# Attention and two MLP layers on one core: the second layer regrouped into 1024, 1024 and 128 tokens

## The chip, the cores and the metric

The kernel runs on one core of a Trainium2 chip. TensorE does the matrix products, VectorE and ScalarE the elementwise work, and the DMA queues of SyncE and ScalarE move data between HBM and the on-chip memory. The metric is the device time of one execution in microseconds (us); lower is better. Three runs of the kernel before gave 831.91 to 832.73 us.

## The reference

Four sequences of 544 tokens (32 global and 512 local) go through attention with 8 heads of 64, and the 2304 rows of 512 through two layers, all in float32:

```python
out_g = sm(scale * q_g @ k_all.T) @ v_all            # 32 global queries see everything
out_l = sm(local window of +-32, and all global) @ v  # 512 local queries
x = concat(out_g, out_l) as (2304, 512)
x = leaky(x @ w_in, alpha) @ w_out                    # layer 1: 512 -> 2048 -> 512
h = x @ moe2_w_in                                     # layer 2: 512 -> 2048 -> 512
return (h * clip(h + 3, 0, 6) / 6) @ moe2_w_out
```

## The kernel before

A float32 product is made of three products of split operands (high times high, low times high, high times low), so each product of 128 by 128 weights is three matmuls, each with its own weight load. The hidden size of 2048 is 16 chunks j of 128; the inner size of 512 is 4 chunks c.

Layer 1 goes over five blocks of tokens, of 512, 512, 512, 256 and 384 columns (`blocks`, line 404); the last one holds a local half of 256 tokens and the 128 global tokens. In each block step s makes the hidden chunk s (`h_tile`, line 443, 12 matmuls), its activation and split (`act`, line 454), and two steps later (`LAG`) its share of the output (`y_tiles`, line 471). In between, `STEPS` (line 42) says how many steps of attention are issued after each step: first all local units, then four global units (line 318: scores `gs_ps`, exponentials, transposes `gpt_ps`, values `go_ps`). At the last step of a block the next block's attention output is transposed and split at once (`x_from_attention`, line 415). `SPLIT` spreads the preparation of layer 2's weights (`second_weights`) over the same blocks: it reads each 64-bit raw weight, makes float32, high and low parts and sums, and stores them to `wi_m` and `wo` in HBM.

Layer 2 (`second_layer`, line 769) takes the tokens in pairs of halves and uses a scheme with seven block products in place of eight. Before, there are two such groups (`twos`, line 632): 512 + 512 tokens and 384 + 384 tokens. For each, eight chunk pairs m run seven products of six matmuls (`product`, line 796, written to `k_ps`, width 512 or 384), and then seven sums over the hidden size (`summed`, line 874, written to `o_ps`, 256 columns each). The last 384 tokens (`rest`, line 633: local half and global tokens of block 4) go through a plain loop (lines 943 to 960): 16 times 12 matmuls of 384 columns and 9 of 512, with weights loaded once more. Weights come through a ring of eight buffers (`ahead`, line 700): six tiles are asked for ahead, and a tile's buffer is free again when its last matmul is done. `more` interleaves the next group's input splits into the sums (`MORE`, line 47).

The order on each engine is written by a scheduler that follows the program's priorities and its own estimate of times; `here` pins single instructions. Engines run their queues in order, SyncE's DMA queue too.

Of the kernel before, what the change touches and what calls it, by code (L numbers as in the profile page):

```python
# [25 lines left out]
W = 32  # L26
# [15 lines left out]
STEPS = [[2] * 4 + [1] * 16, [1] * 16, [1] * 16, [1] * 16, [0] * 16]  # L42
# [14 lines left out]
def fused_kernel(ctx, tc, qkE, vE, qgz, kN, vN, vgN, w1, w2, consts, out):  # L57
# [357 lines left out]
    def x_from_attention(pieces, xt, at):  # L415

        for hp in range(HP):
            t = bank("xt_ps")
            n = 0
            for piece in pieces:  # L420
                x = xo.pop(("g", hp) if piece == "g" else (*piece, hp))
                for i in range(1 if piece == "g" else 2):
                    nc.tensor.transpose(t[:, n:n + 128], x if piece == "g" else x[:, i, :], ident_sb)  # L423
                    n += 128
            split_x(t[:, :n], xt[hp][:, :, at:at + n], n)
# [3 lines left out]
    def active(bi, s):  # L429

        if bi:
            return [(0, width[bi], s)] if s < NJ else []
        if s < DELAY:
            return [(0, 256, s)]
        if s < 2 * DELAY:
            return [(256, 512, s - DELAY)]
        return [(0, 512, s - DELAY)] if s - DELAY < NJ else []
# [5 lines left out]
    def h_tile(xt, wts, parts):  # L443
        ps = bank("h_ps")
        for a, b, j in parts:
            k = 0
            for c in range(NC):
                for wl, xl in ((0, 0), (1, 0), (0, 1)):
                    nc.tensor.matmul(ps[:, a:b], lhsT=wts[j][:, 0, wl, 128 * c:128 * c + 128], rhs=xt[c][:, xl, a:b],  # L449
                                     start=k == 0, stop=k == 3 * NC - 1)  # L450
# [3 lines left out]
    def act(layer, ps, parts):  # L454
# [3 lines left out]
        if layer == 0:  # L458
            nc.scalar.activation(t[:, a:b], ps[:, a:b], AF.Relu, scale=-1.0)  # L459
            for c, d, j in parts:  # L460
# [10 lines left out]
    def y_tiles(layer, y, g, wts, parts, lanes=False):  # L471
        for a, b, j in parts:
# [3 lines left out]
            for (wl, gl), c in steps:  # L476
                first = a == 0 and j == 0 and (wl, gl) == (0, 0)
                last = j == NJ - 1 and (wl, gl) == (0, 1) and (not lanes or b == 512)
                if layer == 0:
                    nc.tensor.matmul(y[c][:, a:b], lhsT=wts[j][:, 1, wl, 128 * c:128 * c + 128], rhs=g[:, gl, a:b],  # L480
                                     start=first, stop=last, skip_group_check=lanes)
# [3 lines left out]

    def evacuate(y, c, n, tags=("t",)):
        r = work.tile([128, 512], F32, tag=tags[c % len(tags)], name="ev", bufs={"t": TB, "z": ZB}[tags[c % len(tags)]])
        if c % 2:
            nc.vector.tensor_copy(r[:, :n], y[:, :n])
        else:  # L490
            nc.scalar.copy(r[:, :n], y[:, :n])
        return r

# [138 lines left out]
    twos = [([(1, 0, 512)], [(2, 0, 512)]), ([(0, 0, 384)], [(0, 384, 128), (3, 0, 256)])]  # L632
    rest = 4
# [15 lines left out]
    def inputs(two, bt, keep=lambda x: x):  # L649
# [13 lines left out]
        for c in range(2):  # L663
# [23 lines left out]
                ("22", (3, 0))]  # L687

    stream = {"todo": [], "got": {}, "n": -1}

    def plan_stream():

        for n in range(len(twos)):
            stream["todo"] += [("in", n, m, kind) for m in range(NP) for kind in (0, 3, 2, 1)]
            stream["todo"] += [("sum", n, i, k) for i in range(len(PRODUCTS)) for k in range(NP // 2)]
        n = len(twos)
        for j in range(NJ + LAG):
            stream["todo"] += [("in", n, j // 2, j % 2)] * (j < NJ) + [("out", n, 0, j - LAG)] * (j >= LAG)

    def ahead(n):  # L700

        while stream["todo"] and len(stream["got"]) < n:
# [8 lines left out]
            if key[0] == "in" and key[1] < len(twos) and key[3] == 1:  # L711
                half = in_parts[key[2]][:, 1].rearrange("p (h c) -> p h c", h=2)[:, :, 256:512]
                nc.sync.dma_start(out=t.bitcast(F32)[:, :, 256:512], in_=half)
            elif key[0] == "in":
                nc.sync.dma_start(out=flat, in_=in_parts[key[2]][:, key[3]])
            elif key[0] == "out":
                nc.sync.dma_start(out=flat, in_=out_parts[:, key[3] // 2, key[3] % 2])
            else:
                kind, half = PRODUCTS[key[2]][1]
# [8 lines left out]
    def act2(src, g, n=512):  # L728
        t = work.tile([128, 512], F32, tag="t", name="t", bufs=TB)[:, 0:n]
        nc.scalar.activation(t, src, AF.Relu, bias=half_sb, scale=1.0 / 6.0)  # L730
        nc.vector.scalar_tensor_tensor(out=t, in0=t, scalar=1.0, in1=src, op0=ALU.min, op1=ALU.mult)
# [245 lines left out]
    for bi in range(len(blocks)):  # L977
# [5 lines left out]
        for s in range(end + LAG):  # L983
# [30 lines left out]
            if last and s >= 2:  # L1014
                next(more, None)
# [77 lines left out]
```

## Time and profile before

| what | us |
|---|---|
| median of 3 runs | 832.2 |
| profiled execution, its own time | 831.75 |
| its span, first to last instruction | 829.9 |
| TensorE busy | 812.1 (98%) |
| VectorE busy | 585.1 (70%) |
| ScalarE busy | 427.4 (51%) |

The span is the profile's clock: times in its rows count from the span's start. Matmul durations overlap in the records, so the time of a run of matmuls is read from the chain, where each piece ends where the next begins. The rows below are named by group in the prediction.

### The profile page before, as it was taken

Reading aid. Unit: us, or ns where it says so; the run is one execution under the profiler, and the core shown is the slowest. Engines: PE = TensorE matmul, PEld = TensorE weight load, DVE = VectorE, ACT = ScalarE, POOL = GpSimd, SP = SyncE. Lnnn points to the kernel's source line nnn. Section 1 sums busy time; section 2 is a strip of 40 time slices with the busy share of each in tenths; the row PEclk is TensorE's granted clock in tenths of the full one; section 3 lists DMA queues with packets and bytes.
Section 4 is the critical chain, followed back from the end, with each engine's and each line's share of the span. In section 5 each row is a group of like instructions: output and inputs, shape, how many; then the busy total and the mean of one; then the engine's idle time right before and its main releaser. Section 6 shows DMA issues by size and latency. Waiting matters only on the chain.

```text
span 829.9 us, 17685 instructions
## 1 busy us (share of the span) xinstructions
PE 812.1 (98%) x6940; PEld 724.3 (87%) x6940; DVE 585.1 (70%) x1283; ACT 427.4 (51%) x929; POOL 0.2 (0%) x4
## 2 busy tenths in 40 slices
PE   6999999999999999999999999999999999999997
PEld 4788888888888888788899988889999999999996
DVE  4998996477878777776688847778857778854221
ACT  5887995445556664465445434434542435532222
POOL 0000000000000000000000000000000000000000
PEclk9899999999999999999999999999999999999999
DMA  9985674347869767787595655666676878788871
GB/s 332 338 282 194 242 255 149 103 180 247 291 233 314 249 239 267 244 316 242 182 291 191 193 187 191 194 214 200 215 242 210 281 248 291 240 285 260 280 253 66
DMA packets 72866, 195.67 MB, mean 236 GB/s; under 512 B 7120, under 2 KB 18384, under 8 KB 72784
## 3 DMA queue, kind: packets, MB, share of 16 engines
q1 hardware_dynamic: 72688, 194.42, 69.5%
q8 instruction: 55, 0.90, 0.5%
q14 instruction: 27, 0.22, 0.1%
q10 hardware_dynamic: 96, 0.13, 0.1%
HBM read 152.05 MB, written 42.47 MB: 234 GB/s over the span
## 4 chain that ended last, share of the span: by engine, by line
PE 92%; ACT 3%; DVE 2%; DMA 2%; issue 0%; SPq 0%; ACTq 0%; DVEq 0%
PE y_ps L480 22%; PE h_ps L449 22%; PE o_ps L884 17%; PE k_ps L801 16%; PE h_ps L953 4%; PE o_ps L739 4%; DMA qk_t<-in_qkE 2%; PE s_ps L208 2%; PE o_ps L254 2%; PE pt_ps L241 1%; ACT p L230 1%; PE xt_ps L423 1%; PE gs_ps L346 1%; PE go_ps L391 1%; DVE z L121 0%; PE gpt_ps L373 0%
## 5 line engine op out<-in xcount | busy, mean ns | idle before, releaser
L480 PE MATMUL y_ps<-g,wt 128*128 128x512 f32 (+2 forms) x1008 | 206.3, 353 | 1.7 <-ACT g L467 1.7
L449 PE MATMUL h_ps<-xt,wt 128*128 128x512 f32 (+2 forms) x1008 | 204.3, 352 | 2.3 <-DVE xt L410 1.5
L449 PEld LDWEIGHTS h_ps<-xt,wt 128*128 128x128 f32 x1008 | 170.1, 191 | 24.7 <-DVE xt L410 2.4
L480 PEld LDWEIGHTS y_ps<-g,wt 128*128 128x128 f32 x1008 | 167.5, 189 | 25.6 <-ACT g L467 2.1
L884 PE MATMUL o_ps<-ws,gh 128*128 128x256 f32 x784 | 139.4, 283 | 0.0
L801 PE MATMUL k_ps<-bt,ws 128*128 128x512 f32 (+1 forms) x672 | 135.1, 362 | 0.0
L801 PEld LDWEIGHTS k_ps<-bt,ws 128*128 128x128 f32 x672 | 121.2, 188 | 13.0
L884 PEld LDWEIGHTS o_ps<-ws,gh 128*128 128x128 f32 x784 | 120.8, 192 | 0.1
L884 PE MATMUL o_ps<-ws,gl 128*128 128x256 f32 x392 | 107.0, 283 | 0.0
L814 ACT CAST gh<-far 128x1024 fp32r<-128x1024 f32 (+1 forms) x56 | 52.8, 942 | 62.5 <-PE o_ps L884 58.2
L815 DVE TENSOR_TENSOR gl<-far,gh 128x1024 fp32r<-128x1024 f32 (+1 forms) x56 | 60.9, 1088 | 33.0 <-ACT gh L814 32.8
L884 PEld LDWEIGHTS o_ps<-ws,gl 128*128 128x128 f32 x392 | 73.5, 192 | 0.0
L461 DVE SCALAR_TENSOR_TENSOR t<-t,c_sb,h_ps 128x512 f32<-128x512 f32 (+2 forms) x84 | 53.5, 641 | 27.9 <-ACT t L459 27.7
L459 ACT ACTIVATE t<-h_ps 128x512 f32<-128x512 f32 (+2 forms) x84 | 42.6, 512 | 45.0 <-PE h_ps L449 43.9
L468 DVE TENSOR_TENSOR g<-t,g 128x512 fp32r<-128x512 f32 (+2 forms) x84 | 49.1, 586 | 21.1 <-ACT g L467 18.6
L467 ACT CAST g<-t 128x512 fp32r<-128x512 f32 (+2 forms) x84 | 45.2, 538 | 35.3 <-DVE t L461 35.0
L786 ACT ACTIVATE t<-far,half_sb 128x512 f32<-128x512 f32 (+1 forms) x48 | 32.2, 671 | 50.8 <-DVE far L782 49.7
L230 ACT ACTIVATE p<-p,st 128x128 f32<-128x128 f32 x128 | 49.6, 390 | 12.6 <-DVE st L226 12.6
L121 DVE SCALAR_TENSOR_TENSOR z<-z,raw 128x512 uint32<-128x512 uint32 x64 | 43.6, 688 | 9.3 <-ACT z L116 6.0
L110 ACT ACTIVATE raw<-raw,quarter_sb 128x512 uint32<-128x512 uint32 x64 | 49.3, 772 | 1.2 <-DMA raw<-in_w 1.2
L123 DVE SCALAR_TENSOR_TENSOR z<-raw,z 128x512 uint32<-128x512 uint32 x64 | 43.4, 688 | 0.7
L953 PE MATMUL h_ps<-xt,ws 128*128 128x384 f32 x192 | 36.0, 336 | 0.0
(101 smaller groups left out, 858.4 us busy)
## 6 DMA issues: line engine op xcount, KB each, us to landing
ws<-wo SPq DMA_DIRECT2D x72, 512.0 KB, 4.2
raw<-in_w SPq DMA_DIRECT2D x64, 512.0 KB, 5.6
ws<-wi SPq DMA_DIRECT2D x64, 512.0 KB, 4.6
v_t<-in_vE SPq DMA_DIRECT2D x32, 512.0 KB, 7.1
qk_t<-in_qkE SPq DMA_DIRECT2D x32, 368.0 KB, 5.0
wi<-raw SPq DMA_DIRECT2D x16, 512.0 KB, 3.1
wi<-parts SPq DMA_DIRECT2D x16, 512.0 KB, 4.6
wo<-raw SPq DMA_DIRECT2D x16, 512.0 KB, 4.2
```

The lines of the kernel that those rows point to most:

```text
L110: here(nc.scalar.activation(low, low, AF.Relu, bias=quarter_sb, scale=0.9 * 2.0 ** -29))
L230: nc.scalar.activation(p[:, n, :], p[:, n, :], AF.Exp, bias=st[:, 1, n:n + 1], scale=-1.0, accum_out=st[:, 2, n:n + 1])
L449: nc.tensor.matmul(ps[:, a:b], lhsT=wts[j][:, 0, wl, 128 * c:128 * c + 128], rhs=xt[c][:, xl, a:b], start=k == 0, stop=k == 3 * NC - 1)
L461: nc.vector.scalar_tensor_tensor(out=t[:, c:d], in0=t[:, c:d], scalar=c1_sb[:, j:j + 1], in1=ps[:, c:d], op0=ALU.mult, op1=ALU.add)
L467: nc.scalar.copy(g[:, 0, a:b], t[:, a:b])
L468: nc.vector.tensor_tensor(out=g[:, 1, a:b], in0=t[:, a:b], in1=g[:, 0, a:b].bitcast(F32), op=ALU.subtract)
L480: nc.tensor.matmul(y[c][:, a:b], lhsT=wts[j][:, 1, wl, 128 * c:128 * c + 128], rhs=g[:, gl, a:b], start=first, stop=last, skip_group_check ...
L801: nc.tensor.matmul(bank, lhsT=wt[:, wl, at:at + 128], rhs=bt[x][:, c, xl, 0:w], start=first and k == 0, stop=k == 5, skip_group_check=True)
L814: nc.scalar.copy(hi, src)
L815: nc.vector.tensor_tensor(out=lo, in0=src, in1=hi.bitcast(F32), op=ALU.subtract)
L884: mm = nc.tensor.matmul(bank, lhsT=part[:, jp, 128 * c:128 * c + 128], rhs=wo[:, jp, 256 * wl:256 * wl + 256], start=opens, stop=k == NP / ...
L953: nc.tensor.matmul(h, lhsT=wt[:, wl, 128 * c:128 * c + 128], rhs=xt[c][:, xl, 0:w], start=k == 0, stop=k == 3 * NC - 1)
```

## The change

Layer 2 now has two groups of 512 + 512 tokens, the second one made of block 0 (512) and of the local halves of batch 3 (256 + 256). Only the 128 global tokens remain (`rest`), and they have no loop of their own: in the second group each chunk pair m, after its products, also multiplies the global tokens by its two unsummed weight tiles (`rest_in`, tokens as stationary operand, 12 matmuls of 256 columns), every second pair ends in an activation, and one pair later four transposes (`rest_turned`) and a split. The unsummed output weights are used during four of the sums (`REST_OF`): three are loaded there anyway, the fourth needs four loads at the end, with the last 24 matmuls (`rest_out`). The weight tiles of kind 0 and 1 are loaded in other pieces (halves of the inner size, runs of 1 KB), in the second group both halves of both.

In layer 1, the block of 256 columns goes in 8 steps of two hidden chunks, with one activation for both; `STEPS` issues three more attention steps in block 2, so the first global unit begins there; and `x_from_attention` is parted: transposes (`x_transposed`) at the block's last step as before, the splits (`x_split`) after its last `y_tiles`.

```diff
-STEPS = [[2] * 4 + [1] * 16, [1] * 16, [1] * 16, [1] * 16, [0] * 16]
+STEPS = [[2] * 4 + [1] * 16, [1] * 16, [1]*11+[2]*3+[1]*2, [2] * 8, [0] * 16]
...
+        if bi and width[bi] == 256:
+            return [(256 * i, 256 * i + 256, 2 * s + i, 0) for i in range(2)] if 2 * s < NJ else []
...
-    twos = [([(1, 0, 512)], [(2, 0, 512)]), ([(0, 0, 384)], [(0, 384, 128), (3, 0, 256)])]
-    rest = 4
+    twos = [([(1, 0, 512)], [(2, 0, 512)]), ([(0, 0, 512)], [(3, 0, 256), (4, 0, 256)])]
+    rest = x2[4][:, :, 256:384]
...
+    REST_OF = {0: (0, 0), 2: (1, 0), 4: (1, 1), 7: (0, 1)}
...
+            if key[0] == "in" and key[3] < 2:
+                own = in_parts[key[2]][:, 0:2].rearrange("p j (h t c) -> p (j h) t c", h=2, t=2)[:, :, key[3]]
+                n = 2 if key[3] == 0 and key[1] + 1 < len(twos) else 4
+                nc.sync.dma_start(out=flat.rearrange("p (jh c) -> p jh c", jh=4)[:, 0:n], in_=own[:, 0:n])
...
+        def rest_in(m, wts):
+            if m % 2 == 0:
+                hr["h"] = kept("hr_ps")
+            to = hr["h"].rearrange("p (m j k) -> p m j k", m=2, j=2)[:, m % 2]
+            k = 0
+            for c in range(NC):
+                for wl, xl in ((0, 0), (1, 0), (0, 1)):
+                    w = own_parts(wts[c // 2])[:, :, wl, 128 * (c % 2):128 * (c % 2) + 128]
+                    nc.tensor.matmul(to, lhsT=xr[0][:, xl, 128 * c:128 * c + 128], rhs=w, start=m % 2 == k == 0,
+                                     stop=k == 3 * NC - 1, skip_group_check=True)
+                    k += 1
...
+        def rest_turned(m):
+            t = kept("tr_ps")
+            for i in range(4):
+                nc.tensor.transpose(t[:, 128 * i:128 * i + 128], hr["t"][:, 128 * i:128 * i + 128], ident_sb)
+            split_x(t, gr[m // 2], 512)
+        def rest_out(y, i, k, wo):
+            kind, half = REST_OF[i]
+            for jp in range(2):
+                j = 2 * (2 * k + jp) + kind
+                for wl, gl in ((0, 0), (1, 0), (0, 1)):
+                    mm = nc.tensor.matmul(y[:, 256 * half:256 * half + 256],
+                                     lhsT=gr[j // 4][:, gl, 128 * (j % 4):128 * (j % 4) + 128],
+                                     rhs=wo[:, jp, 256 * wl:256 * wl + 256], start=i == k == jp == wl == gl == 0,
+                                     stop=i in (2, 7) and k == NP // 2 - 1 and jp == gl == 1, skip_group_check=True)
...
-            product(b0, 1, "21", ka, False)
+            b1 = take("in", n, m, 1)
+            product(b1, 0, "21", ka, False, True)
-            b1 = take("in", n, m, 1)
-            product(b1, 1, "t4", kc, False)
+            product(b1, 1, "t4", kc, False, True)
...
+                if end:
+                    if m and m % 2 == 0:
+                        rest_turned(m - 1)
+                    rest_in(m, (b0, b1))
...
+                    if end and i == k == 0:
+                        rest_turned(NP - 1)
+                    if end and i in REST_OF:
+                        rest_out(yr, i, k, wo)
...
-        n, w = len(twos), width[rest]
-        y = [kept("o_ps") for _ in range(w // 128)]
...
+            if end:
+                for k in range(NP // 2):
+                    rest_out(yr, len(PRODUCTS), k, take("sum", n, len(PRODUCTS), k))
+                rest_rows(yr, 1)
...
-                x_from_attention(blocks[bi + 1], xt_next, 0)
+                coming = x_transposed(blocks[bi + 1], 512 // width[bi + 1])
...
+            if s == end + LAG - 1 and not last:
+                x_split(coming, xt_next, 0)
```

TensorE's order at the start of the second group's products stands first (`k_ps` products, `hr_ps` the global tokens' hidden part, `tr_ps` its transposes). Before, the end of the first group's sums (`o_ps`) and then one run of products:

```order
L884 MATMUL o_ps<-ws,gh 128x256 x2
L884 MATMUL o_ps<-ws,gl 128x256
L801 MATMUL k_ps<-bt,ws 128x384 x328
L884 MATMUL o_ps<-ws,gh 128x256 x2
L884 MATMUL o_ps<-ws,gl 128x256
```

And after:

```order
L816 MATMUL k_ps<-bt,ws 128x512 x4
L768 MATMUL hr_ps<-ws,xr 128x256 x2
L816 MATMUL k_ps<-bt,ws 128x512 x6
L768 MATMUL hr_ps<-ws,xr 128x256 x16
L816 MATMUL k_ps<-bt,ws 128x512 x18
L768 MATMUL hr_ps<-ws,xr 128x256 x6
L816 MATMUL k_ps<-bt,ws 128x512 x24
L780 MATMUL tr_ps<-consts_sb,tr 128x128 x4
```

The global tokens' matmuls stand between the products, and the second pair's (the last 12 of the first 24) even stand ahead of all of that pair's own products.

VectorE's order at the end of block 1 (`xt` the next block's splits, `z`, `raw` and `parts` the weight preparation, `ev` the copies of block 1's output). Before:

```order
L410 TENSOR_TENSOR xt_3215<-xt_ps_3225,xt_3215 128x512
L410 TENSOR_TENSOR xt_3216<-xt_ps_3232,xt_3216 128x512
L410 TENSOR_TENSOR xt_3217<-xt_ps_3239,xt_3217 128x512
L548 TENSOR_TENSOR raw_3047<-z_3092,raw_3047 128x512
L113 TENSOR_SCALAR z_3260<-raw_3055 128x512
L1025 COPY ev_3321<-y_ps_2137 128x512
L121 SCALAR_TENSOR_TENSOR z_3260<-z_3260,raw_3055 128x512
```

And after:

```order
L121 SCALAR_TENSOR_TENSOR z_3252<-z_3252,raw_3055 128x512
L123 SCALAR_TENSOR_TENSOR z_3252<-raw_3055,z_3252 128x512
L410 TENSOR_TENSOR xt_3215<-xt_ps_3223,xt_3215 128x512
L549 TENSOR_TENSOR raw_3055<-z_3252,raw_3055 128x512
L410 TENSOR_TENSOR xt_3216<-xt_ps_3228,xt_3216 128x512
L558 TENSOR_TENSOR z_3252<-z_3252 128x256
L410 TENSOR_TENSOR xt_3217<-xt_ps_3233,xt_3217 128x512
L558 TENSOR_TENSOR z_3252<-z_3092,z_3252 128x256
L1039 COPY ev_3321<-y_ps_2137 128x512
L1039 COPY ev_3326<-y_ps_2139 128x512
```

The three later splits now have weight preparation ahead of them and between them.

TensorE's order where the first global unit runs. Before, in the block of 256 columns:

```order
L449 MATMUL h_ps<-xt,wt 128x256 x12
L480 MATMUL y_ps<-g,wt 128x256 x24
L373 MATMUL gpt_ps<-consts_sb,gp 128x128 x4
L374 MATMUL gpt_ps<-consts_sb,gp 32x128
L449 MATMUL h_ps<-xt,wt 128x256 x12
L373 MATMUL gpt_ps<-consts_sb,gp 128x128 x4
```

And after, in block 2:

```order
L490 MATMUL y_ps<-g,wt 128x512 x12
L459 MATMUL h_ps<-xt,wt 128x512 x12
L490 MATMUL y_ps<-g,wt 128x512 x15
L373 MATMUL gpt_ps<-consts_sb,gp 128x128 x4
L490 MATMUL y_ps<-g,wt 128x512 x6
L374 MATMUL gpt_ps<-consts_sb,gp 32x128
L459 MATMUL h_ps<-xt,wt 128x512 x12
L373 MATMUL gpt_ps<-consts_sb,gp 128x128 x4
```

Between a unit's scores and its first transposes there are now 39 matmuls of 512 columns, where there were 36 of 256.

## Rows read from the trace of the kernel before

**Rows 1.** The page: span, and each engine's busy time

```profile
span 829.9 us, 17685 instructions
...
PE 812.1 (98%) x6940; PEld 724.3 (87%) x6940; DVE 585.1 (70%) x1283; ACT 427.4 (51%) x929; POOL 0.2 (0%) x4
```

**Rows 2.** Chain that ended last, in order of time: start us, us, what

```profile
240.70 1.31 PE xt_ps L423 x12
...
484.04 74.62 PE k_ps L801 x329
558.65 69.11 PE o_ps L884 x576
...
640.66 56.86 PE k_ps L801 x328
697.52 51.83 PE o_ps L884 x432
...
766.31 2.10 PE h_ps L953 x12
768.42 2.08 PE o_ps L739 x9
...
818.66 6.18 PE o_ps L739 x27
```

**Rows 3.** Busy time by stretch: sums of group 1, products of group 2

```profile
559.00:629.00 70.00, 70.00 (x583) 70.00 (x582) 53.98 (x57) 33.12 (x40) 0.00 (x0) 1.00 0.68 215
...
640.00:698.00 58.00, 58.00 (x340) 58.00 (x339) 44.31 (x82) 25.44 (x46) 0.00 (x0) 1.00 0.83 274
```

**Rows 4.** Timeline of TensorE, 330 to 420 us, all its waits in brackets

```profile
352.98 1.71 PE L480 MATMUL y_ps<-g,wt 128*128 128x256 f32 x12 [1.47 <-ACT g L467]
...
355.61 1.69 PE L449 MATMUL h_ps<-xt,wt 128*128 128x256 f32 x12 [0.37 <-DVE gst L360]
357.65 0.66 PE L373 MATMUL gpt_ps<-consts_sb,gp 128*128 128x128 f32 x4 [0.36 <-ACT gp L361]
```

**Rows 5.** Timeline, 228 to 256 us: TensorE, then VectorE

```profile
245.76 5.61 PE L449 MATMUL h_ps<-xt,wt 128*128 128x512 f32 x24
...
238.11 0.75 DVE L260 TENSOR_TENSOR xo<-o_ps,rs 128x256 f32<-128x256 f32 x2
...
241.80 1.89 DVE L410 TENSOR_TENSOR xt<-xt_ps,xt 128x512 fp32r<-128x512 f32 x3 [0.76 <-ACT xt L409]
243.60 0.68 DVE L548 TENSOR_TENSOR raw<-z,raw 128x512 fp32r<-128x512 f32 x1
244.20 0.42 DVE L113 TENSOR_SCALAR z<-raw 128x512 f32<-128x512 f32 x1
```

**Rows 6.** Timeline of the end, all engines

```profile
824.46 1.07 ACT L491 COPY ev<-o_ps 128x512 f32<-128x512 f32 x2 [3.99 <-PE o_ps L739]
824.86 0.69 DVE L489 COPY ev<-o_ps 128x512 f32<-128x512 f32 x1 [3.80 <-PE o_ps L739]
...
825.07 0.87 ACTq L751 DMA_DIRECT2D out<-ev  x2
825.96 0.88 SPq L755 DMA_DIRECT2D out<-ev  x2
```

**Rows 7.** DMA issues, 484 to 830 us: KB each, median us to landing

```profile
out<-res SPq DMA_DIRECT2D x28, 128.0 KB, 3.8
...
out<-ev SPq DMA_DIRECT2D x2, 256.0 KB, 2.3
...
out<-ev ACTq DMA_DIRECT2D x2, 64.0 KB, 2.0
```

**Rows 8.** Line 715, loads of whole input weight tiles: last line

```profile
DMA to landing us min/median/max: 3.1/4.6/8.3
```

**Rows 9.** Groups by line and shape: us, mean ns, idle before

```profile
L884 PEld LDWEIGHTS o_ps<-ws,gl 128*128 128x128 f32 x392 | 73.5, 192 | 0.0
...
L658 DVE TENSOR_TENSOR bt<-xt,bt 128x512 fp32r<-128x512 f32 x8 | 5.4, 683 | 0.1
...
L658 DVE TENSOR_TENSOR bt<-xt,bt 128x384 fp32r<-128x384 f32 x8 | 4.4, 552 | 1.2 <-ACT bt L657 1.2
...
L1024 ACT COPY ev<-y_ps 128x256 f32<-128x256 f32 x2 | 0.8, 380 | 1.3 <-PE y_ps L480 1.3
```

More of the change, by code (lines that the diff above doesn't have):

```diff
@@ L1 @@
 from contextlib import ExitStack
-from itertools import islice
+from itertools import chain, islice
 import numpy as np
@@ L694, in plan_stream @@
             stream["todo"] += [("in", n, m, kind) for m in range(NP) for kind in (0, 3, 2, 1)]
[L695 to L698, printed above, removed]
+            last = n + 1 == len(twos)
+            stream["todo"] += [("sum", n, i, k) for i in range(len(PRODUCTS) + last) for k in range(NP // 2)]
     def ahead(n):
@@ L726, in take @@
         return stream["got"].pop(key)
[L728 to L731, printed above, removed]
-        nc.scalar.copy(g[:, 0, :], t)
-        nc.vector.tensor_tensor(out=g[:, 1, :], in0=t, in1=g[:, 0, :].bitcast(F32), op=ALU.subtract)
-    def outputs(y, g, wo, j, order=None):
-        wo = wo.rearrange("p h (two c) -> p two h c", two=2)
-        for c in order or range(len(y)):
-            for wl, gl in ((0, 0), (1, 0), (0, 1)):
-                nc.tensor.matmul(y[c].rearrange("p (h c) -> p h c", h=2), lhsT=g[:, gl, 128 * c:128 * c + 128],
-                                 rhs=wo[:, wl],
-                                 start=j == 0 and (wl, gl) == (0, 0), stop=j == NJ - 1 and (wl, gl) == (0, 1))
@@ L790, in second_layer, with rest_rows @@
+        def rest_rows(y, half):
+            at = slice(256 * half, 256 * half + 256)
+            r = work.tile([128, 512], F32, tag="z", name="rz", bufs=ZB)[:, 0:256]
+            nc.scalar.copy(r, y[:, at])
+            for b in range(B):
+                queue = nc.scalar if b % 2 else nc.sync
+                queue.dma_start(out=rows[b, 0:SG, at], in_=r[W * b:W * b + W, :])
         for n, two in enumerate(twos):
@@ L794, in second_layer, with product @@
             far = []
-            def product(wt, half, x, bank, first=True):
+            def product(wt, half, x, bank, first=True, own=False):
+                wt = own_parts(wt)[:, half] if own else wt[:, :, 256 * half:256 * half + 256]
                 k = 0
@@ L835, in second_layer @@
             coming, split = operands(), []
+            if end:
+                first = wp.tile([128, 2, 2, 512], F32R, tag="w", name="gr", bufs=NJ)
+                gr += [first[:, 0], first[:, 1]]
+                gr += [later["xs"].tile([128, 2, 512], F32R, tag="xq", name="gr", bufs=3) for _ in range(2)]
             for m in range(NP):
@@ L864, in second_layer @@
                 act2_in(g21, g21)
[L866 to L872 removed]
+                if end:
+                    if m and m % 2 == 0:
+                        rest_turned(m - 1)
+                    rest_in(m, (b0, b1))
+            bt_next, more = {}, iter(())
+            if not end:
+                more = chain(inputs(twos[n + 1], bt_next, here), rest_inputs(xr))
             def summed(i, y, first=True):
@@ L910, in second_layer @@
             x_, y_ = total(kept), total(fresh)
+            yr = kept("yr_ps") if end else None
             summed(0, x_)
```

134 lines of the change are left out of this document (50 added, 84 removed).

## The prediction

> **What bounds the kernel now.** I read the page first. TensorE is busy for 812.1 of the 829.9 us, VectorE for 70%, ScalarE for 51% [rows 1]. That alone does not say that TensorE sets the end, so next comes the chain of waits: from 484.04 us to the last matmul it is one unbroken succession of TensorE pieces, each starting where the one before it ends [rows 2]. Then the stretches of layer 2: in the sums of group 1 and the products of group 2 TensorE is busy in all of 70.00 and all of 58.00 us at a granted clock of 1.00, while VectorE has 77% and 76% and the DMA engines 68% and 83% [rows 3]. So in layer 2 a matmul taken out counts in full, and other engines' work counts only if it arrives late. In layer 1, between 330 and 420 us, TensorE waits three times, all at the first global unit, for 1.47, 0.37 and 0.36 us [rows 4]. After the last matmul (818.66 + 6.18 = 824.84, [rows 2]) 5.06 us of copying and storing are left to the span's end.
>
> The prices of TensorE come from the chain, since pieces there do not overlap [rows 2]: a matmul of 512 columns 74.62 / 329 = 0.227 us, of 384 columns 56.86 / 328 = 0.173 (as `h_ps` of the last loop, 2.10 / 12 = 0.175), of 256 columns 69.11 / 576 = 0.120, in group 2 also 51.83 / 432 = 0.120; 512 columns taken in two pieces 2.08 / 9 = 0.231; a transpose of 128 columns 1.31 / 12 = 0.109. The price follows the columns, with some 10 ns on top at 256.
>
> **Layer 2's matmuls.** Before: 336 products of 512 (76.2 us), 672 sums of 256 (80.6), 336 products of 384 (58.3), 504 sums (60.5), and the last loop, 192 of 384 (33.6) and 144 of 512 in two pieces (33.3): 342.5 us. After: two groups of 76.2 + 80.6 = 156.8, so 313.7, then for the global tokens 96 matmuls of 256 columns on the inside and 96 towards the output, 192 x 0.120 = 23.0, and 16 transposes, 1.75: 338.4 us. The sevenths saved on 256 more tokens outweigh the narrower form of the global tokens: **-4.0 us**. The 96 on the inside read the weights in two pieces of 128 columns; 512 in two pieces cost 0.004 us more than whole, so 96 x 0.004 = 0.4 us is the upper bound of that, none the lower; I take 0.1, which leaves **-3.9**. Weight loads grow too, since 256-column matmuls have one each as well; in the sums, where loads take 192 ns each [rows 9] and one is needed every 120 ns, PEld is busy for 70.00 of 70.00 us [rows 3] and the spacing is still 0.120, so I count none of it extra.
>
> **What VectorE gets in return.** The splits of group 2's inputs go from 552 to 683 ns [rows 9], 16 or so of them, 2 us within the sums of group 1, and the global tokens add one split there; VectorE has 70.00 - 53.98 = 16 us free in that stretch [rows 3]. In the second group the second halves of four activations and of four splits, 512 columns each, are new, about 8 x 0.65 = 5 us over 157. Cost 0; without cover it would be 2 us at the boundary of the groups.
>
> **The end.** Before, after 824.84 us, two copies of ScalarE from 824.46 and one of VectorE from 824.86 (0.69) run, issues follow at 825.07, and SyncE's last pair begins at 825.96 [rows 6], landing 2.3 us after issue [rows 7]. After, the last 24 matmuls (2.9 us) belong to 256 columns of one bank: one copy of 256 columns, 0.38 us [rows 9], then four small stores, two on either queue, landing in about 2.0 [rows 7]. The issue of SyncE could come some 0.9 us sooner, that is 825.96 - 825.07. The sums' last stores of 128 KB land in 3.8 us [rows 7] and now have these 2.9 us over them. Bounds: 0 (a store still queued ahead) to -1.5 (both shorter steps in full); I take **-0.8**.
>
> **The first global unit.** Its 2.2 us of waits [rows 4] came where 36 matmuls of 256 columns (36 x 0.120 = 4.3 us) covered its exponentials. In block 2, 39 matmuls of 512 columns stand there, 8.8 us, so the wait for `gp` should go. New ones can come: the scores' second bank on an activation of the hidden chunk, the transposes on the exponentials, the scores on their keys. The nearest row for the largest is the 1.47 us of before. Lower bound: all 2.2 us go. Upper: 2.2 us at each of four units in place of 2.2 once, +6.6. I take **-0.5**, near the lower end's half, since only one unit waited before although all four had the same thin cover. The steps of two chunks hold the same matmuls in the same widths; nothing is counted for them.
>
> **The splits apart.** VectorE ends the three later splits of a block's inputs at 241.80 + 1.89 = 243.7 us, TensorE's first matmul of the next block starts at 245.76 [rows 5]. In the new order weight preparation stands ahead of and between these splits. From 238.11 + 0.75 the work up to the last split comes to 6.8 us: four splits of 0.63, two preparation steps at 0.68 and two at 0.42 [rows 5], and three others that I put at 0.68 at most. It ends at 245.7, and the last split is needed only 9 matmuls (2.0 us) after the block's start. Cost 0. Uncovered it would be 4 x 0.63 = 2.5 us at three boundaries, 7.6 us.
>
> **The weights of group 2.** Each pair loads four whole tiles, 2.1 MB, in 42 x 0.227 + 12 x 0.120 = 11.0 us: 191 GB/s, where the same stretch moved 274 before [rows 3]. Loads therefore have more room on average, though in pieces of 1 KB. The critical point is the order: odd pairs' global matmuls stand ahead of their own products, so both tiles are needed at the pair's start; the second was first needed after 30 of its pair's 42 matmuls. The tile's buffer comes free with the last product two pairs earlier, 11.0 us sooner; the worst landing of a whole tile is 8.3 [rows 8]. Cost 0, with 2.7 us to spare.
>
> **Sum** on the profiled execution: 831.75 - 3.9 - 0.8 - 0.5 = 826.55. The median of the runs stands 0.45 above that execution, so 827.0.
>
> **Rivals.** (1) The global units' waits come back: 2.2 us at three of the four units instead of one adds 4.4 and loses the 0.5: 827.0 + 0.5 + 4.4 = 831.9, no change. For it: the units now run between wide matmuls whose activations share ScalarE; against: the longer cover.
>
> (2) On the slower side: the odd pairs' second tile is late. If the three loads of the pair land one after another at the median 4.6 us [rows 8], the second tile is there after 13.8 us, 2.8 after it is needed, in four odd pairs: +11.3, 838.3. It decides (slower than before by its measure) from (1.7 + 5.2) / 4 = 1.7 us late per odd pair on. For it: the order, and one queue in sequence. Against: 274 GB/s was reached in the same stretch before, at which three tiles (1.57 MB) take 5.7 us.
>
> (3) TensorE's time goes by the number of matmuls more than by columns: layer 2 has 2224 instructions of TensorE instead of 2184; at the mean 342.5 / 2184 = 0.157 us the change would be +6.3 in place of -3.9, 827.0 + 10.2 = 837.2. Against it: 0.120 and 0.227 stand side by side for 256 and 512 columns in one trace [rows 2]. The Trainium skill ("TensorE: Matmul & The Clock Gate", section "Back-to-back issue gap") has a sustained spacing of 81 ns at 128 columns and 131 ns at 512, much flatter than the trace; by a straight line between the two (an estimate from that page), layer 2's matmuls would cost 1.3 us more after the change and the total would be 832.2. The trace disagrees, with 227 ns at 512, and the sum goes by the trace.
>
> (4) All waits of the global units go and the tail gains fully: 831.75 - 3.9 - 2.2 - 1.5 + 0.45 = 824.6.
>
> **How the numbers follow.** A measurement of this kernel can tell 0.2% from no change, 1.7 us: faster means below 830.5, slower above 833.9. The forecast has 0.70, with its own range of 825.4 to 829.6 (tail at 0, some waits kept); rival 1 has 0.14, rival 2 0.07, rival 3 0.03, rival 4 0.06. Faster: 0.70 + 0.06, and 0.02 of rival 1 in which only one further unit waits: 0.78. Same: the remaining 0.12 of it. Slower: 0.10. The range takes in rivals 4 and 1 and leaves out 2 and 3: 824.4 to 832.0.
>
> **What the new profile would show.** Right: products of each group about 76 us and sums 81 us in the chain, `hr_ps` and `yr_ps` at 0.120 each without idle time ahead, less than 2.2 us of waits of `gpt_ps` and `gs_ps` in blocks 2 and 3, a first matmul of each block that waits for no split, and less than 4.6 us from the last matmul to the span's end. Wrong: idle time of TensorE until a DMA to `ws` ahead of `hr_ps` or `k_ps` (rival 2), waits for `gp` or the activation at each unit (rival 1), a spacing of `hr_ps` well above 0.125 us (rival 3), or h matmuls at a block's start waiting for `xt`, which would make the splits' cost of 0 wrong.

## The result and the profile after

The changed kernel takes 825.18 us (median of 5 runs, 823.27 to 826.15) where the kernel before took 832.73 on the same chip (831.91 to 833.73): a ratio of 0.9905, 95% interval 0.989 to 0.9919, or 7.9 us less. The forecast was 827.0, some 5 us less, with a range of 824.4 to 832.0. The direction holds, and so does the stated range; the forecast's own, narrower range of 825.4 to 829.6 is missed by 0.2 us. Two terms of the sum do not have their size.

The page of the profile after, span and engines, answers to [rows 1]:

```profile
span 821.5 us, 17564 instructions
...
PE 809.2 (99%) x6980; PEld 714.1 (87%) x6980; DVE 596.6 (73%) x1247; ACT 423.3 (52%) x886; POOL 0.2 (0%) x4
```

The chain that ended last, after (start us, us, what), answers to [rows 2]:

```profile
479.64 74.62 PE k_ps L816 x329
554.25 69.11 PE o_ps L904 x576
...
639.28 1.92 PE hr_ps L768 x16
641.20 4.14 PE k_ps L816 x18
...
739.28 14.40 PE o_ps L904 x120
...
814.49 2.89 PE yr_ps L789 x24
```

TensorE's pieces again follow each other to the end. Products and sums of group 1 have the very durations of before, the global tokens' matmuls of 256 columns cost 1.92 / 16 = 0.120 us inside and 2.89 / 24 = 0.120 at the end, and TensorE's rows of layer 2 have no wait in brackets. So 0.120 and 0.227 us by width hold for the new forms too, but for small amounts that the section on the prediction counts.

To see where the time went, three marks cut the span: the first matmul of block 2's hidden chunks, the first of the 329 products, and the end of the last matmul. Block 2 begins at 245.76 before [rows 5]; after, the timeline of TensorE has it here:

```profile
244.72 5.61 PE L459 MATMUL h_ps<-xt,wt 128*128 128x512 f32 x24
```

| stretch, us | before | after | difference | forecast |
|---|---|---|---|---|
| start to block 2 | 245.76 | 244.72 | -1.04 | 0 |
| block 2 to group 1's products | 238.28 | 234.92 | -3.36 | -0.5 |
| products to the last matmul | 340.80 | 337.74 | -3.06 | -3.9 |
| last matmul to the span's end | 5.06 | 4.12 | -0.94 | -0.8 |
| span | 829.9 | 821.5 | -8.4 | -5.2 |

The first line is scatter: in the profiled executions of all kernels below, block 2 begins between 244.7 and 248.8 us, and the code up to there hardly differs. The other stretches repeat within some 0.3 us as long as their code stays, so a stretch tells what a median of four to six runs, which spread over 1 to 4 us, can't.

**The middle stretch** gained almost seven times its forecast. The waits of [rows 4] are gone, all 2.2 us: TensorE's timeline of 325 to 410 us has no bracket. The rest is in the scores of the global units (`gs_ps`). Each unit has eight such matmuls, two heads times four batches, each on 64 rows by 32 columns of the array (64*32 in the rows), and each counts as two instructions, so x16 is all eight. Timeline of TensorE before, units 1, 2 and 4:

```profile
347.11 1.09 PE L346 MATMUL gs_ps<-gk,gq 64*32 64x512 f32 x16
...
363.02 1.06 PE L346 MATMUL gs_ps<-gk,gq 64*32 64x512 f32 x8
...
364.45 1.06 PE L346 MATMUL gs_ps<-gk,gq 64*32 64x512 f32 x8
...
396.32 1.06 PE L346 MATMUL gs_ps<-gk,gq 64*32 64x512 f32 x8
...
397.98 1.06 PE L346 MATMUL gs_ps<-gk,gq 64*32 64x512 f32 x8
```

And after:

```profile
324.65 1.09 PE L346 MATMUL gs_ps<-gk,gq 64*32 64x512 f32 x16
...
352.76 1.66 PE L346 MATMUL gs_ps<-gk,gq 64*32 64x512 f32 x16
...
368.87 1.44 PE L346 MATMUL gs_ps<-gk,gq 64*32 64x512 f32 x16
...
382.76 1.06 PE L346 MATMUL gs_ps<-gk,gq 64*32 64x512 f32 x8
...
385.14 1.06 PE L346 MATMUL gs_ps<-gk,gq 64*32 64x512 f32 x8
```

Eight matmuls together take as long as four: about 1.0 us. Before, units 2 to 4 (the third, left out, is like the others) had theirs in two halves with output matmuls between, 1.0 + 3 x 2.0 = 7.0 us, as the scheduler placed them; after, units 2 and 3 have them undivided, with only a short hold inside (to the next instruction 1.6 and 1.4 us), and unit 4 in halves: 1.0 + 1.6 + 1.4 + 2.0 = 6.0. In unit 3 the second head's weight loads start at 369.22 us, just after VectorE's last read of a hidden chunk's bank (368.23 + 0.88 = 369.11); in unit 2 they start at 353.33, after a read that ends at 353.21. So the hold is probably the wait for that bank, which no run shows by an edit. That is -1.0; with the 2.2 it makes 3.2 of the 3.36. That these two nearly make up the whole is in part luck: the block's 256-column matmuls, in fewer runs, took another 1.1 us less, and the first unit's pieces among block 2's wide matmuls 1.2 more (the table at the end of the experiments).

**The end**, after, from the timeline of all engines, answers to [rows 6]:

```profile
817.40 0.37 ACT L800 COPY rz<-yr_ps 128x256 f32<-128x256 f32 x1 [9.27 <-PE yr_ps L789]
817.80 1.00 SPq L803 DMA_DIRECT2D out<-rz  x2
817.80 0.84 ACTq L803 DMA_DIRECT2D out<-rz  x2
```

One copy of 0.37 us, then two stores on either queue at once, as forecast. In ten of the kernels below this end took 3.4 to 3.7 us, so the gain is more often 1.5 than 0.9 (the old end took 5.06 and 5.09 in the two traces that have it).

### The profile page after: what moved, and what is told of

Its sections match the earlier page's. It is cut to its first block, busy times and chain, and to the rows that moved or that the text cites. A ratio compares the mean times of both kernels' runs of the same rounds, so it can differ in the third digit from the quotient of the medians.

```text
span 821.5 us, 17564 instructions
## 1 busy us (share of the span) xinstructions
PE 809.2 (99%) x6980; PEld 714.1 (87%) x6980; DVE 596.6 (73%) x1247; ACT 423.3 (52%) x886; POOL 0.2 (0%) x4
## 4 chain that ended last, share of the span: by engine, by line
PE 93%; DVE 2%; ACT 2%; DMA 1%; SPq 1%; issue 0%; DVEq 0%; ACTq 0%
PE y_ps L490 23%; PE h_ps L459 22%; PE o_ps L904 20%; PE k_ps L816 19%; PE s_ps L208 2%; PE o_ps L254 2%; PE yr_ps L789 1%; PE hr_ps L768 1%; DMA raw<-in_w 1%; PE pt_ps L241 1%; ACT p L230 1%; PE go_ps L391 1%; PE xt_ps L426 1%; PE gs_ps L346 1%; DVE z L121 1%
## 5 line engine op out<-in xcount | busy, mean ns | idle before, releaser
L904 PE MATMUL o_ps<-ws,gh 128*128 128x256 f32 x896 | 160.9, 283 | 0.1
L816 PE MATMUL k_ps<-bt,ws 128*128 128x512 f32 x672 | 157.2, 390 | 0.0
L816 PEld LDWEIGHTS k_ps<-bt,ws 128*128 128x128 f32 x672 | 124.6, 188 | 24.9
L904 PEld LDWEIGHTS o_ps<-ws,gh 128*128 128x128 f32 x896 | 138.8, 192 | 0.6 <-issue 0.3
L904 PE MATMUL o_ps<-ws,gl 128*128 128x256 f32 x448 | 124.2, 283 | 0.0
L830 DVE TENSOR_TENSOR gl<-far,gh 128x1024 fp32r<-128x1024 f32 x56 | 68.5, 1223 | 42.3 <-ACT gh L829 42.3
L829 ACT CAST gh<-far 128x1024 fp32r<-128x1024 f32 x56 | 58.7, 1048 | 74.4 <-PE o_ps L904 70.6
L904 PEld LDWEIGHTS o_ps<-ws,gl 128*128 128x128 f32 x448 | 84.9, 192 | 0.0
L750 ACT ACTIVATE t<-far,half_sb 128x512 f32<-128x512 f32 x48 | 34.8, 724 | 77.1 <-DVE far L746 77.1
L751 DVE SCALAR_TENSOR_TENSOR far<-t,far 128x512 f32<-128x512 f32 x48 | 33.1, 689 | 11.8 <-ACT t L750 11.8
```

What stands on the lines that cost most here:

```text
L816: nc.tensor.matmul(bank, lhsT=wt[:, wl, 128 * c:128 * c + 128], rhs=bt[x][:, c, xl, 0:w], start=first and k == 0, stop=k == 5, skip_group_ ...
L829: nc.scalar.copy(hi, src)
L830: nc.vector.tensor_tensor(out=lo, in0=src, in1=hi.bitcast(F32), op=ALU.subtract)
L904: mm = nc.tensor.matmul(bank, lhsT=part[:, jp, 128 * c:128 * c + 128], rhs=wo[:, jp, 256 * wl:256 * wl + 256], start=opens, stop=k == NP / ...
```

## The experiments

Each ratio is to the kernel before, run on the same chip. "The middle" is the stretch from block 2 to group 1's products in the table above.

**Layer 1's changes alone.** The kernel before with the new attention steps, two-chunk steps and parted splits.

```diff
-STEPS = [[2] * 4 + [1] * 16, [1] * 16, [1] * 16, [1] * 16, [0] * 16]
+STEPS = [[2] * 4 + [1] * 16, [1] * 16, [1]*11+[2]*3+[1]*2, [2] * 8, [0] * 16]
...
-                x_from_attention(blocks[bi + 1], xt_next, 0)
+                coming = x_transposed(blocks[bi + 1], 512 // width[bi + 1])
...
```

> The kernel before with the changes to layer 1 alone (two-chunk steps, attention steps sooner, splits apart); layer 2 as before. Theory: what layer 1 gained in the trace, 3.4 us between 325 and 411 us, is real and independent of layer 2, so about 3.4 below the kernel before (829.3 against 832.7), TensorE's first products of layer 2 some 3.4 us sooner, and the end of the program as before. Rival, the prediction's own term: -0.5, no more than 832.2, the rest of the trace's difference being the scatter of the program's start.

**Layer 2's change alone.** The changed kernel with those lines taken back.

```diff
-STEPS = [[2] * 4 + [1] * 16, [1] * 16, [1]*11+[2]*3+[1]*2, [2] * 8, [0] * 16]
+STEPS = [[2] * 4 + [1] * 16, [1] * 16, [1] * 16, [1] * 16, [0] * 16]
...
-        if bi and width[bi] == 256:
-            return [(256 * i, 256 * i + 256, 2 * s + i, 0) for i in range(2)] if 2 * s < NJ else []
...
-                coming = x_transposed(blocks[bi + 1], 512 // width[bi + 1])
+                x_split(x_transposed(blocks[bi + 1]), xt_next, 0)
...
```

> The changed kernel with layer 1 in the old form (single chunks in the 256-column block, attention steps as before, splits with the transposes); layer 2 regrouped. Theory: layer 2's matmuls -3.1 and the end -0.95, so about 4.0 below the kernel before (828.7), with the waits of the first global unit (2.2 us) and its three score batches in halves still there. Rival: the regrouping carries nearly all of the gain (825 to 826), because layer 1's part of the trace difference is scatter.

Measured: layer 1 alone 828.66, ratio 0.9957 (0.9946 to 0.9969), by it 3.6 us less; layer 2 alone 827.79, ratio 0.9949 (0.9936 to 0.9961), 4.2 us less. Together 7.8, and both at once gave 7.9; within these intervals of about 1 us either way the parts are independent. The stretches agree more closely: with layer 1 alone the middle takes 479.91 - 245.03 = 234.88 us and layer 2 340.80, as before; with layer 2 alone it takes 238.54, and layer 2 337.72. Chain of the first, then of the second kernel:

```profile
479.91 74.62 PE k_ps L811 x329
...
814.53 6.18 PE o_ps L749 x27
```

```profile
487.38 74.62 PE k_ps L814 x329
...
822.21 2.89 PE yr_ps L787 x24
```

The theory holds in both runs, and both rivals fall: layer 1's part is real, and the regrouping carries little more than half of the gain.

**The first global unit in the 256-column block again.**

```diff
-STEPS = [[2] * 4 + [1] * 16, [1] * 16, [1]*11+[2]*3+[1]*2, [2] * 8, [0] * 16]
+STEPS = [[2] * 4 + [1] * 16, [1] * 16, [1] * 16, [2] * 8, [0] * 16]
```

> The changed kernel with one attention step per step in block 2, so that the first global unit begins in the 256-column block; two-chunk steps stay. Theory A (beginning the first unit sooner removed its waits): the waits come back, and as only 24 matmuls of 256 columns (2.9 us) now stand between the first scores and their transposes, TensorE waits 2 to 3 us there; all four score batches stand undivided, worth 1.0 us for the fourth; sum +1 to +2, 826.2 to 827.2. Theory B (two-chunk steps removed the waits): no wait, and the undivided fourth batch gives -1.0, 824.2.

Measured: 825.72, ratio 0.9918 (0.9906 to 0.9931), a little under the 826.2 to 827.2 of theory A; middle 237.34, 2.4 more than in the changed kernel. Theory A holds on the waits: 1.42, 0.31 and 0.37 us. Timeline of TensorE, and the windows behind it (stretch, its length, busy time of TensorE, weight loads, VectorE, ScalarE, POOL, granted clock, DMA share, GB/s):

```profile
348.24 1.09 PE L346 MATMUL gs_ps<-gk,gq 64*32 64x512 f32 x16
...
351.01 1.22 PE L490 MATMUL y_ps<-g,wt 128*128 128x256 f32 x8 [1.42 <-ACT g L477]
352.53 3.63 PE L490 MATMUL y_ps<-g,wt 128*128 128x256 f32 x16 [0.31 <-DVE g L478]
```

```profile
352.00:353.00 1.00, 0.69 (x5) 0.49 (x5) 1.00 (x2) 0.15 (x1) 0.00 (x0) 0.86 0.97 373
353.00:354.00 1.00, 1.00 (x6) 1.00 (x6) 0.96 (x4) 0.00 (x0) 0.00 (x0) 0.50 0.99 331
...
356.00:357.00 1.00, 0.76 (x6) 0.48 (x4) 0.20 (x1) 0.31 (x1) 0.00 (x0) 0.93 1.04 342
```

None of the expectations had the second part: after these waits the granted clock was 0.50 (1.2 in place of 2.4 GHz) for some 3 us, and 16 matmuls of 256 columns took 3.4 us (352.53 to 355.97, where the next instruction begins) instead of 1.9. In the kernel before, the waits of [rows 4], of much the same length, left the clock at 1.00; its window behind the first of them:

```profile
352.00:354.00 2.00, 1.02 (x8) 1.02 (x9) 1.81 (x7) 1.47 (x4) 0.00 (x0) 1.00 0.98 341
```

What tells the two cases apart no run shows. All four score batches stand undivided here at 1.0 us each, which gives back 1.9.

**Single-chunk steps in the 256-column block.**

```diff
-STEPS = [[2] * 4 + [1] * 16, [1] * 16, [1]*11+[2]*3+[1]*2, [2] * 8, [0] * 16]
+STEPS = [[2] * 4 + [1] * 16, [1] * 16, [1]*11+[2]*3+[1]*2, [1] * 16, [0] * 16]
...
-        if bi and width[bi] == 256:
-            return [(256 * i, 256 * i + 256, 2 * s + i, 0) for i in range(2)] if 2 * s < NJ else []
...
```

> The changed kernel with the 256-column block in single-chunk steps again, one attention step each; the first unit still begins in block 2. Theory A (sooner start removed the waits): no wait at the first unit, but the third score batch is divided again (two halves of four matmuls at 1.0 us each in place of one batch), +0.6 to +1.0: 825.8 to 826.2. Theory B (two-chunk steps did it): waits of about 2.2 us at the units in the block, 827.4 or more.

Measured: 826.04, ratio 0.9924 (0.9912 to 0.9935), middle 236.55, 1.6 more than in the changed kernel. Only one wait came back, at the second unit:

```profile
361.24 0.66 PE L373 MATMUL gpt_ps<-consts_sb,gp 128*128 128x128 f32 x4 [0.70 <-ACT gp L361]
```

The score batches stood as 8, 8, 4 + 4, 4 + 4, 6.0 us in all, as in the changed kernel. So theory A has the right number, but for another reason. The other 0.9 us of the 1.6 lie in the block's 256-column matmuls (`h_ps` and `y_ps`), which stand in 40 runs here and in 25 in the changed kernel: 49.24 us against 48.32, from the start of each run to the start of what follows.

**Splits straight behind the transposes**, first in the changed kernel, later in the kernel with undivided batches (below).

```diff
-                coming = x_transposed(blocks[bi + 1], 512 // width[bi + 1])
+                x_split(x_transposed(blocks[bi + 1], 512 // width[bi + 1]), xt_next, 0)
...
-            if s == end + LAG - 1 and not last:
-                x_split(coming, xt_next, 0)
```

> The changed kernel with each block's input splits straight behind their transposes, as before. By the prediction's step (splits apart cost and gain nothing) the boundaries of blocks 1 to 2 and 2 to 3 stay as they are, within 0.2 us. In this kernel's order the third score batch is divided too, which by the theory of undivided batches costs 0.4 to 1.0 us: 825.6 to 826.2. Rival: the parting was what kept VectorE's queue free at the boundaries, so idle TensorE time until xt appears there, 0.6 us or more at each of three: 827 or more.

> The kernel with undivided score batches, with the splits straight behind the transposes again. In the run with the splits together, TensorE waited 1.1 us for an activation in the 256-column block, and a batch was divided; here no batch is divided. Theory (the prediction's step: parting the splits is worth nothing by itself): within 0.3 us of the kernel with undivided batches. Rival (parted splits keep ScalarE's and VectorE's queues free where the first unit's exponentials run): 1 to 2 us slower than it, with waits for g or xt in the 256-column block.

Measured: 826.29, ratio 0.9935 (0.9923 to 0.9947), middle 237.30, that is +2.4; and with undivided batches 823.81 (ratio 0.9894, 0.9877 to 0.991), middle 234.00 against 233.71. The first kernel has a wait within the 256-column block, not at a block's start:

```profile
363.17 1.22 PE L490 MATMUL y_ps<-g,wt 128*128 128x256 f32 x8 [1.08 <-ACT g L477]
```

and its third batch in halves (0.6 more); the rest is small amounts in several places (table below). In the second kernel a wait for `gp` grew from 0.17 to 0.48 us. With undivided batches on both sides the parting is thus worth 0.3 us, hardly more than a stretch scatters; most of the 2.4 comes with the order in which the scheduler then put the global units.

**Scores pinned in program order**, second head first.

```diff
-                for h in range(2):
-                    nc.tensor.matmul(s[h][W * b:W * b + W, :], lhsT=q[64 * h:64 * h + 64, h, W * b:W * b + W],
-                                     rhs=k[64 * h:64 * h + 64, b, 0:SL], start=True, stop=True)
+                for h in (1, 0):
+                    mm = nc.tensor.matmul(s[h][W * b:W * b + W, :], lhsT=q[64 * h:64 * h + 64, h, W * b:W * b + W],
+                                          rhs=k[64 * h:64 * h + 64, b, 0:SL], start=True, stop=True)
+                    here(mm)
```

> The changed kernel with the 8 score matmuls of each global unit kept in program order, second head first. The fourth unit's batch now stands as 1 and 7 instead of 4 and 4. Theory (matmuls of the two heads and the four batches run side by side in the array, so a batch costs 1.0 us however many of the eight it holds): no gain in the fourth, 1.9 us again, since it still stands in two pieces; the second and third stay at 1.4 to 1.6 us or shrink to 1.0 if the order of heads held them up: 824.2 to 825.2. Rival (each matmul has its own price): the fourth as 1 and 7 costs the same sum as 4 and 4, and the first piece alone takes 0.25 us instead of 1.0.

Measured: 823.78, ratio 0.9905 (0.9893 to 0.9917), the same as the changed kernel. The fourth unit's batch settles what a batch costs:

```profile
383.70 1.04 PE L346 MATMUL gs_ps<-gk,gq 64*32 64x512 f32 x2
...
386.42 1.08 PE L346 MATMUL gs_ps<-gk,gq 64*32 64x512 f32 x14
```

One matmul alone takes as long as seven (0.97 and 1.01 us, up to the next instruction). The theory of matmuls side by side holds, the price by the piece falls. Units 2 and 3 keep their 1.6 and 1.4 us, so the order of the heads is not what holds them.

**One weight buffer less in layer 2.**

```diff
-STREAM = 3
+STREAM = 2
```

> The changed kernel with seven weight buffers for layer 2 instead of eight, five tiles asked ahead instead of six. The prediction said that the tiles have 2.7 us to spare in group 2's odd pairs; one buffer less takes about a quarter of a pair, 2.7 us, so by it the loads are at the edge: 825.2 to 827. If the slack were larger (the rival to it), no change, 825.2; if the loads were already at the edge, TensorE waits for ws about 2.7 us in each of four odd pairs or more, 836 or more.

Measured: 824.08, ratio 0.9905 (0.9891 to 0.992), layer 2 in 337.65 us, no wait. In the changed kernel's trace every tile of group 2's products lands within 5.4 us of its issue, where the prediction took 8.3 as the worst: by the same sum the room was 11.0 - 5.4 = 5.6 us instead of 2.7, and a loss of 2.7 stays covered. Rival 2 is far off.

**One transfer a queue at the end**, with the pinned scores.

```diff
-            for b in range(B):
-                queue = nc.scalar if b % 2 else nc.sync
-                queue.dma_start(out=rows[b, 0:SG, at], in_=r[W * b:W * b + W, :])
+            for b in range(0, B, 2):
+                queue = nc.scalar if b else nc.sync
+                queue.dma_start(out=rows[b:b + 2, 0:SG, at], in_=r[W * b:W * b + 2 * W, :])
```

> The changed kernel with the score matmuls in program order and the last rows stored by one transfer on either queue (two batches each) instead of two. Theory: the second transfer's issue on SyncE (0.5 us) leaves the end, 0.4 to 0.5 us less from the last matmul to the span's end (3.6 us instead of 4.1), and the scores' part as in the run with the scores alone: 823.8 to 824.8. Rival: the end is set by the landing of one transfer, whatever their number, no change: 824.2 to 825.2.

Measured: 827.32, ratio 0.9943 (0.9931 to 0.9955): 3.2 us slower than the pinned scores alone by the ratios, and both expectations fall. The end takes 6.28 us instead of 3.50. Its DMA view from 819 us to the end (share in 40 slices, GB/s), and the changed kernel's from 817 us:

```profile
DMA  8100000000011011211111111111110000000000
GB/s 293 29 0 0 0 0 0 0 0 0 6 23 12 18 47 35 88 41 12 41 47 29 47 47 53 41 59 47 47 47 12 0 0 0 0 0 0 0 0 0
```

```profile
DMA  9710000000000675347600000000000000000000
GB/s 369 254 41 0 0 0 0 0 0 0 0 0 0 164 205 148 74 115 189 164 25 16 16 0 0 0 0 0 0 0 0 0 0 0 0 0 0 0 0 0
```

About a tenth to a fifth of the DMA engines worked at a time instead of 0.3 to 0.7 of them; the same bytes took some 3.7 us instead of 1.2. The edit changed the number of transfers and their pattern (the pair of batches is now the outermost dimension) together, and no run tells which of the two did it.

**Undivided score batches**, from one doubled attention step less in block 2. **Global tokens' matmuls in whole runs**, by pinning them. And both.

```diff
-STEPS = [[2] * 4 + [1] * 16, [1] * 16, [1]*11+[2]*3+[1]*2, [2] * 8, [0] * 16]
+STEPS = [[2] * 4 + [1] * 16, [1] * 16, [1]*11+[2]*2+[1]*3, [2] * 8, [0] * 16]
```

```diff
-                    nc.tensor.matmul(to, lhsT=xr[0][:, xl, 128 * c:128 * c + 128], rhs=w, start=m % 2 == k == 0,
-                                     stop=k == 3 * NC - 1, skip_group_check=True)
+                    mm = nc.tensor.matmul(to, lhsT=xr[0][:, xl, 128 * c:128 * c + 128], rhs=w, start=m % 2 == k == 0,
+                                          stop=k == 3 * NC - 1, skip_group_check=True)
+                    here(mm)
```

> The changed kernel with two fewer doubled attention steps in the other sense: block 2 issues 11 single, 2 double and 3 single steps instead of 11, 3 and 2. In its order all four score batches stand undivided, and 48 matmuls of 256 columns (5.8 us) stand between the scores of units 2 to 4 and their transposes. Theory (a batch costs 1.0 us however many of the eight matmuls it holds, and 5.4 us of cover was enough in the run with the later start): four batches at 1.0 instead of 6.0 us in all, so the stretch from block 2's first matmul to group 1's products goes from 234.9 to 233.0 us, and the time to 822.3 to 823.5. Rival (the doubled steps are what hides the units): waits for g or gp return, 234.9 us or more, 825 or more.

> The changed kernel with the 12 matmuls of the global tokens of each pair kept in program order, so that they stand in 8 runs of 12 instead of 18 runs of 1 to 16 among the products. Layer 2's stretch was 0.8 us longer than the prediction's sum, with products at 0.229 us instead of 0.227 where runs are short. Theory (each change of width costs some 0.03 us): 337.7 us from group 1's products to the last matmul become 337.2 to 337.4, the time 0.3 to 0.5 less, too little for the runs to tell. Rival (the excess comes from loads or from weights read in two pieces): 337.7, unchanged. If the rearranged order made the tiles late, idle time of TensorE ahead of hr_ps or k_ps.

> Both edits of the two runs before it: undivided score batches and the global tokens' matmuls in whole runs. If the two are independent, the sum of both: 2.2 to 2.4 us below the changed kernel, 822 to 823.2; if they are not, no better than the first alone.

Measured: 822.98 (ratio 0.9885, 0.987 to 0.99), 823.55 (0.9894, 0.9879 to 0.9908) and 822.93 (0.9886, 0.9871 to 0.9901). Undivided batches shorten the middle to 479.61 - 245.90 = 233.71, 1.2 us less; three of the four batches, and the only bracket there:

```profile
331.28 1.09 PE L346 MATMUL gs_ps<-gk,gq 64*32 64x512 f32 x16
...
355.79 1.09 PE L346 MATMUL gs_ps<-gk,gq 64*32 64x512 f32 x16
...
364.02 3.13 PE L459 MATMUL h_ps<-xt,wt 128*128 128x256 f32 x24 [0.17 <-ACT gp L361]
...
388.26 1.09 PE L346 MATMUL gs_ps<-gk,gq 64*32 64x512 f32 x16
```

The batches give 1.9 and 0.17 goes to the wait. Part is lost where the units' transposes (`gpt_ps`) and values (`go_ps`) now stand: the two heads' values come one after the other in units 2 to 4; in unit 2:

```profile
367.62 0.65 PE L391 MATMUL go_ps<-gv,gpt 128*32 128x64 f32 x32
...
368.45 0.65 PE L391 MATMUL go_ps<-gv,gpt 128*32 128x64 f32 x32
```

A head takes 0.83 us, two 1.66; together, as in the changed kernel, they took 1.38 (367.49 to 368.87). Three units make 0.8, of which the first unit, less cut up, gives 0.6 back; the transposes cost 0.95 more, and the 256-column matmuls, in 16 runs, 0.7 less. Whole runs of the global tokens' matmuls took layer 2 to 337.61, only 0.13 less, where 0.3 to 0.5 was expected:

```profile
637.83 9.36 PE k_ps L817 x40
...
680.57 1.43 PE hr_ps L768 x12
682.00 5.47 PE k_ps L817 x24
...
689.33 13.63 PE k_ps L817 x60
```

That does not refute the theory of 0.03 us for each broken run. The products stand in 8 runs instead of 22, and seven of them still take 0.02 to 0.03 us more than their number at 0.227 (5.47 for 24 is 5.44 + 0.03). But the first run of 40 takes 9.36 instead of 9.07, because a weight load waits 0.41 us at 638.7, by the trace for ScalarE's copy `ab` (line 868). So 0.29 us of the gain went into a new hold. Both edits together: middle 233.63, layer 2 337.62, the sum of the two, 1.4 us instead of the 2.2 to 2.4 expected. By the stretches the kernel with undivided batches beats the changed one by 1.2 us; their ratios' intervals overlap.

**Where the middle's time went.** TensorE's timeline of the middle, each run counted from its start to the start of the next, without the waits in brackets; in parentheses the number of runs. The last four columns are experiments from above.

| us | before | after | unit 1 in 256-column block | single-chunk steps | splits straight behind | undivided batches |
|---|---|---|---|---|---|---|
| waits | 2.20 | 0 | 2.10 | 0.70 | 1.08 | 0.17 |
| score batches (64*32) | 6.97 | 5.97 | 4.07 | 6.00 | 6.48 | 4.08 |
| `h_ps`, `y_ps`, 256 columns | 49.46 (40) | 48.32 (25) | 49.25 (19) | 49.24 (40) | 48.76 (29) | 47.58 (16) |
| `h_ps`, `y_ps`, 512 columns | 88.56 | 89.20 | 88.47 | 89.19 | 89.18 | 88.96 |
| `gpt_ps` | 3.67 | 3.62 | 4.73 | 3.40 | 3.72 | 4.57 |
| `go_ps` | 5.56 | 6.11 | 6.63 | 6.12 | 6.35 | 6.36 |
| all else | 81.86 | 81.70 | 82.09 | 81.90 | 81.73 | 81.99 |
| middle | 238.28 | 234.92 | 237.34 | 236.55 | 237.30 | 233.71 |

With unit 1 in the 256-column block, the 256-column row holds the stretch at half the clock, some 1.5 us.

## Why the prediction was right, and where it was not

- **TensorE bounds the kernel, and its matmuls cost by their columns: right.** Forecast -3.9 for layer 2, measured -3.06. The durations of each form are as forecast, so the mechanism is right and the size 0.8 too large. The missing 0.8 lies in group 2: from the end of group 1's sums (625.21 + 11.51 = 636.72) to the last matmul (817.38) it takes 180.7 us, where the sum by its 328 remaining products, 672 sums, 192 matmuls of the global tokens and 16 transposes gives 179.8. The chain, read piece by piece, has it:

```profile
656.90 2.75 PE k_ps L816 x12
...
802.74 11.74 PE o_ps L904 x96
```

The global tokens' matmuls cut the products into 22 runs, each about 0.03 us above its number at 0.227 (12 take 2.75 instead of 2.72), 0.66 in all; their own runs stay 0.14 below their price. Ahead of the last 96 sums comes a hold of 0.34 (0.11 without work from 802.63, then 11.74 where group 1 has 11.51); what holds them stays open. The prediction allowed 0.1 us for the split weight tiles, which cost nothing, and nothing for the broken runs of products. Rival 3 would have lost time here, and layer 2 gained 3.06 us. By the flatter spacing of the Trainium skill ("TensorE: Matmul & The Clock Gate", "Back-to-back issue gap") layer 2 would, in the prediction's estimate, have lost 1.3 us. This trace does not agree: it has 0.227 us at 512 columns and 0.120 at 256 in the new forms too.
- **The end: right,** -0.94 in this trace, -1.3 to -1.6 in the ten others with the new end, against -0.8 with a bound of -1.5.
- **The first global unit: the step that failed in size.** The prediction took -0.5, "near the lower end's half". The whole of the lower end, -2.2, is what came. The longer cover it had itself worked out, 8.8 us against 4.3, was no reason to expect another wait. That starting the unit sooner is what removed the waits is shown, since the later start brought all three back. But the prediction gave the thin cover of the exponentials as their reason, and only 0.36 of the 2.2 was a wait for `gp`. The largest, 1.47, was for `g`, the activation of a hidden chunk. In the kernel before, VectorE took up its part of that activation at 352.02 us, behind a unit's maxima (`gst`) and weight preparation in its queue, though ScalarE's part had ended at 351.26:

```profile
350.18 0.68 DVE L357 TENSOR_REDUCE gst<-gs_ps 128x1 f32<-128x512 f32 x1
...
352.02 0.47 DVE L461 SCALAR_TENSOR_TENSOR t<-t,c_sb,h_ps 128x256 f32<-128x256 f32 x1
```

- **"The steps of two chunks hold the same matmuls in the same widths; nothing is counted for them": failed.** Taken back alone, they cost 1.6 us: 0.9 because the block's matmuls stand in 40 runs instead of 25, and a wait of 0.70 at the second unit. The 1.0 us of the score batches is not theirs by itself, since the batches took 6.0 us with single chunks too; what counts is the order that either change brings. The prediction counted matmuls and never asked which of them share the array and what breaks their runs; the timeline of before showed the first, 16 instructions in 1.0 us beside 8 in 1.0.
- **The splits apart, cost 0: right** at the boundary. After, the last split ends 0.2 us ahead of block 2's first matmul.
- **The weights of group 2, cost 0: right,** even with a buffer less. Rival 1 (waits at three units) didn't come; rival 4 in the middle did.

The shares of the layers, 3.6 and 4.2 us by the ratios, show why the total came within 2 us of the median: layer 2's matmuls were forecast 0.8 us too large a gain, layer 1's part 2.9 too small. That the one error took back some of the other is luck.

## What to carry to other kernels

Price small matmuls by the group that shares the array and not one by one, and look in the order for groups that other matmuls cut in two, and for long runs that small ones break. Where the work that covers a wait doubles, count the wait as gone, but look at the next place: with single chunks one of 0.70 us came up at the next unit. Compare executions by stretches between marks: here the start alone scatters by 4 us, as much as the larger part of the change was worth.

## What the runs showed of the hardware

- Score matmuls of 64 rows by 32 columns, 512 columns each: 1, 4, 7 or 8 of them take 0.97 to 1.02 us alike, up to the next instruction, where nothing holds them.
- Runs of 512-column products between 256-column matmuls took about 0.03 us each more than their number at 0.227.
- Waits of 1.42 and 0.31 us in one kernel were followed by a granted clock of 0.50 for 3 us; in the kernel before, 1.47, 0.37 and 0.36 us left it at 1.00.
- A store of 64 rows of 1 KB from two batches, one on either queue: 6.28 us from the last matmul to the end; the same rows as two stores a queue: 3.4 to 4.1.
